# Pooled attention with two gated MLPs on one core: single steps moved in a written order of 2840 steps

## The chip, the cores and the metric

The program runs on one core of one Trainium2 chip. The metric is device time in microseconds (us) from launch to end. The core has a matrix engine (TensorE, PE in the profile), a vector engine (VectorE, DVE), a scalar engine (ScalarE, ACT), a general engine (GpSimd, POOL) and SyncE (SP), which here only issues DMAs. Each works through its own list of instructions; semaphores tie the lists together.

## The reference

q, k and v are 8 batches x 8 heads x 576 tokens x 64. Softmax attention over 8-fold pooled keys and values is followed by two gated MLPs:

```python
k_p = k.reshape(B, H, Sp, pool, D).mean(axis=3); v_p = ...   # 576 keys become 72
x = softmax(scale * q @ k_p^T) @ v_p                          # to (8, 576, 512)
h = np.maximum(x @ w_in, 0.0)                                 # 512 -> 1024
conv_out = 3-tap convolution of h along the tokens            # conv_w
x2 = (h * sigmoid(conv_out)) @ w_out                          # 1024 -> 512
h = gelu(x2 @ w_in2); u, v = h[..., :512], h[..., 512:]       # 512 -> 1024
v_s = einsum('ts,bsd->btd', w_sg, layer_norm(v) * g_ln) + b_sg
out = x2 + (u * v_s) @ w_out2                                 # 512 -> 512
```

All of it is fp32. Some weights arrive as 64-bit words, which DVE turns into fp32.

## The kernel before

Nearly every matrix product is made of three matmuls: each fp32 operand is split into a high part (a cast on ACT) and a low part (a subtraction, line L154, on POOL or DVE), and high x high, low x high and high x low are added in PSUM.

The work is written as small Python generators ("tasks"), and each `yield` ends a step of one to a dozen instructions. A key names a task: a letter, an index, and for most a batch or chunk after the dot. The text `ORDER` (line 23) holds 2840 keys; the last loop walks it and advances the named task by one step each time:

```python
for key in ORDER.split():
    step(key)
```

`step` also ties each new instruction to the one before it on the same engine, so each engine's list is exactly what `ORDER` gives. An instruction whose input is late holds all that stands behind it on its engine.

The tasks of which this text speaks; `X:n` means step n of task X:

- `s(t,b)`: scores of token tile t, batch b. PE (L438), a POOL memset of two columns of `e` (L445, step 1), DVE maximum and subtraction in two halves (L449, L454), ACT exp (L459), DVE sum (L461), POOL normalisation (L476, L480), then a DMA to DRAM.
- `e(t,b)`: the transposed probabilities. For b of 2 and more: DMA back, DVE transpose (L518), ACT cast `eTh` (L522), POOL subtraction `eTl` (L154, step 3), and DVE for a remainder. `a(p,b)`: probabilities times V (PE L117 into `psa`, ACT L550, DVE L552). `V(b)`: pooled V, of which step 3 is the ACT cast `VR` (L384). `k`, `v`: pooling on POOL (L271 to L275). `q`, `p`, `K`: loads and transposes.
- `I(f,c)`: first matmul of hidden block f (0 to 7) and token chunk c (0 to 11, 384 tokens each): 12 matmuls into a `psi` bank (L117); ACT relu and centre tap (L577, L587); DVE other taps (L589, L590); ACT tanh (L592); DVE `g` (L596); ACT cast `hg` (L599); POOL subtraction `hg` (L154). There are two `psi` banks, taken in turn, so a block's matmuls wait for `g` of the block two before it.
- `O(f,c)`: second matmul, 9 matmuls into three `pso` banks (L110 to L112). With f = 7 the banks are emptied by ACT (L623), DVE (L621), ACT, and stored to `x2s` in DRAM.
- `i`, `t`, `w`, `l`: weight blocks of the four matrices. Each is a DMA, three DVE conversions (L166, L169, L172), an ACT cast (L229) and a subtraction (L154, POOL or DVE).
- `g(i)`: block i of `w_sg`: two DMAs into `wn` (L652, L653), two PE transposes into `psa` (L659), each with an ACT cast `w2sh` (L664) and a DVE subtraction `w2sl` (L154). The last is `g4`.
- `y`, `r`: transposes of x2 for the second MLP; `n`: its v half (L760 to L769), first `n0.0`; `u`: its u half; `d`: spatial product; `m`: residual load; `o`: output product (lines from L835).

By time: chunks c = 0 and 1 with the loading of all weights run to about 155 us; chunks and batches then overlap to 575 us; the second MLP runs from there.

Of the kernel before, what the change touches and what calls it, by code (L numbers as in the profile page):

```python
# [26 lines left out]
def pooled_attention_gated_mlps(  # L27
# [25 lines left out]
    B, H, S, D = q.shape  # L53
# [46 lines left out]
    def ps_tile():  # L100
        return ps2["p"].tile([128, 2, 512], F32, tag="ps", name="ps")
# [7 lines left out]
    def mm3(out_, ah, al, bh, bl, first, last):  # L109
        nc.tensor.matmul(out=out_, lhsT=ah, rhs=bh, start=first, stop=False)  # L110
        nc.tensor.matmul(out=out_, lhsT=al, rhs=bh, start=False, stop=False)  # L111
        nc.tensor.matmul(out=out_, lhsT=ah, rhs=bl, start=False, stop=last)  # L112
# [120 lines left out]
    wi, wo, wo2, w2 = {}, {}, {}, {}  # L233
# [478 lines left out]
    g2 = {}  # L712
# [16 lines left out]
    def rows(dst, b, tiles, buf):  # L729

        if tiles[0] < NM:
            r = dst[b][128 * tiles[0]:128 * tiles[-1] + 128, :].rearrange("(j p) d -> p j d", p=128)
            return [(buf[:, 0:len(tiles), :], r)]
        return [(buf[REM * e:REM * e + REM, 0, :], dst[b - 1 + e][128 * NM:S, :]) for e in range(2)]
# [7 lines left out]
    def tiles_of(i):  # L742
        return list(range(2 * i, min(2 * i + 2, NM + 1)))
# [81 lines left out]
    ress = {}  # L825
# [9 lines left out]
    def t_o2(i, b):  # L835
        tiles = tiles_of(i)
        res = ress.pop((b, i))
        ps = ps_tile()
        for j, i in enumerate(tiles):
            T = slice(128 * i, 128 * i + 128)  # L840
            for f in range(NU):
                mm3(ps[:, j, :], g2["gh"][:, f, T], g2["gl"][:, f, T], wo2[f][:, 0, :], wo2[f][:, 1, :],
                    f == 0, f == NU - 1)
        yield
        nt = len(tiles)
        ob = outp.tile([128, 2, 512], F32, tag="ob", name="ob")
        nc.vector.tensor_tensor(out=ob[:, 0:nt, :], in0=ps[:, 0:nt, :], in1=res[:, 0:nt, :], op=ALU.add)
        yield
        for s_, d in rows([out[bb * S:bb * S + S, :] for bb in range(B)], b, tiles, ob):
            nc.sync.dma_start(out=d, in_=s_)  # L850
# [11 lines left out]
    def step(key):  # L862

        if key not in running:
            i, _, b = key[1:].partition(".")
            running[key] = iter(tasks[key[0]](int(i or 0), int(b or 0)) or ())
        more = next(running[key], 0)
        issued = nc.cur_bb.bb.instructions
        for n in range(seen[0], len(issued)):
            ins = issued[n]  # L870
            if ins.engine in last:
                tc.add_manual_dep(ins, last[ins.engine], pin, reason="order")
            last[ins.engine] = ins.name
        seen[0] = len(issued)
        return more is None

    for key in ORDER.split():
        step(key)
# [30 lines left out]
```

## Time and profile before

| | us |
|---|---|
| median of 3 runs | 1011.91 |
| lowest and highest of these | 1010.51 and 1012.82 |
| profiled execution, device time | 1010.28 |
| profiled execution, span from first to last instruction | 1008.5 |
| PE busy in the span | 960.3 (95%) |
| DVE, ACT, POOL busy | 661.7, 466.9, 371.3 |

The profile has one record for each instruction with its start, its duration, and, where its engine sat idle before it, how long and which instruction of another engine ended the wait. A duration of a PE record includes its way through the array, so the pace of PE is the distance between starts. PEclk, or the granted clock, is the share of TensorE's full 2.4 GHz that it had in a stretch; a half is 1.2 GHz.

### The profile page before, as it was taken

What the parts mean: (1) busy time and instruction counts of PE and PEld (TensorE: products, weight loads), DVE (VectorE), ACT (ScalarE), POOL (GpSimd) and SP (SyncE); (2) the same over time, 40 slices, a digit from 0 to 9 for tenths busy, and PEclk for the clock granted to TensorE, in tenths of its full rate; (3) what the DMA queues carried; (4) which work ended last, traced back from release to release, by engine and by line L of the source; (5) the groups of instructions that cost most, each with busy time, mean ns of one, the idle gap of its engine ahead of it and who ended that gap; (6) DMA issues with size and microseconds to landing.
All of it is one profiled execution on the core that took longest, in us unless ns stands there. A gap on an engine that the chain in (4) does not pass through costs nothing.

```text
span 1008.5 us, 15021 instructions
## 1 busy us (share of the span) xinstructions
PE 960.3 (95%) x5473; PEld 865.7 (86%) x5473; DVE 661.7 (66%) x1190; ACT 466.9 (46%) x908; POOL 371.3 (37%) x485
## 2 busy tenths in 40 slices
PE   5798899999998999999899899999999999999997
PEld 4687689889897898988899789898989898989896
DVE  5979986978777587796488676456364626373433
ACT  3666566777766567676456443222132313131120
POOL 3688787678777576474122100001000100010000
PEclk9899999999999999999999999999999999999999
DMA  9945273555638245141820823324141323132112
GB/s 240 308 158 95 79 173 102 124 160 137 178 100 161 75 135 138 47 126 32 230 74 1 235 55 47 107 37 107 30 109 32 76 70 88 45 64 74 42 42 63
DMA packets 210150, 105.81 MB, mean 105 GB/s; under 512 B 161472, under 2 KB 180188, under 8 KB 210076
## 3 DMA queue, kind: packets, MB, share of 16 engines
q1 hardware_dynamic: 210076, 104.85, 41.2%
q8 instruction: 43, 0.70, 0.3%
q14 instruction: 31, 0.25, 0.1%
HBM read 75.33 MB, written 29.49 MB: 104 GB/s over the span
## 4 chain that ended last, share of the span: by engine, by line
PE 76%; DVE 3%; POOL 2%; issue 2%; ACT 1%; DMA 1%; SPq 0%; POOLq 0%; DVEq 0%; ACTq 0%
PE ps L123 22%; PE psi L117 14%; PE ps L110 6%; PE ps L111 6%; PE ps L112 6%; PE pso L110 5%; PE pso L112 5%; PE pso L111 5%; PE psa L117 3%; PE psa L438 2%; DMA eds<-en 1%; POOL eTl L154 1%; POOL hg L154 1%; DVE psi L589 1%; ACT eTh L522 0%
## 5 line engine op out<-in xcount | busy, mean ns | idle before, releaser
L769 POOL TENSOR_SCALAR rstd<-mv 128x2 f32<-128x2 f32 (+1 forms) x20 | 8.9, 446 | 371.8 <-DVE mv L766 371.8
L154 POOL TENSOR_TENSOR hg<-g,hg 128x384 fp32r<-128x384 f32 x96 | 98.2, 1025 | 123.0 <-ACT hg L599 120.4
L815 DVE SCALAR_TENSOR_TENSOR y<-ps,coef,bsg 128x576 f32<-128x576 f32 x32 | 26.1, 816 | 116.2 <-PE ps L123 116.2
L589 DVE SCALAR_TENSOR_TENSOR psi<-h,coef,psi 128x384 f32<-128x384 f32 x96 | 58.6, 611 | 55.3 <-ACT psi L587 55.1
L123 PE MATMUL ps<-w2sh,v 128*128 128x288 f32 x512 | 94.3, 296 | 0.0
L820 ACT CAST gt<-y 128x576 fp32r<-128x576 f32 (+2 forms) x48 | 23.0, 512 | 117.8 <-DVE y L817 117.8
L123 PEld LDWEIGHTS ps<-w2sh,v 128*128 128x128 f32 x512 | 77.1, 189 | 0.0
L577 ACT ACTIVATE h<-psi 128x386 f32<-128x386 f32 (+1 forms) x96 | 47.2, 492 | 62.9 <-PE psi L117 62.6
L592 ACT ACTIVATE psi<-psi 128x384 f32<-128x384 f32 x96 | 45.2, 472 | 46.3 <-DVE psi L590 46.2
L154 POOL TENSOR_TENSOR eTl<-xb,eTh 128x512 fp32r<-128x512 f32 (+1 forms) x30 | 50.4, 1679 | 40.4 <-ACT eTh L522 39.1
L590 DVE SCALAR_TENSOR_TENSOR psi<-h,coef,psi 128x384 f32<-128x384 f32 x96 | 59.8, 623 | 3.4
L599 ACT CAST hg<-g 128x384 fp32r<-128x384 f32 x96 | 48.3, 506 | 26.2 <-DVE g L596 22.2
L438 PE MATMUL psa<-KBT,qT 128*128 128x144 f32 (+1 forms) x320 | 54.7, 302 | 5.5 <-DVE KBT L317 1.5
L596 DVE SCALAR_TENSOR_TENSOR g<-psi,h 128x384 f32<-128x384 f32 x96 | 52.0, 544 | 10.3 <-ACT psi L592 6.9
L587 ACT ACTIVATE psi<-h,coef 128x384 f32<-128x384 f32 x96 | 56.3, 586 | 3.1
L438 PEld LDWEIGHTS psa<-KBT,qT 128*128 128x128 f32 (+1 forms) x320 | 46.4, 187 | 12.1 <-ACT qT L420 2.5
L123 PE MATMUL ps<-w2sl,v 128*128 128x288 f32 x256 | 54.8, 296 | 0.0
L801 ACT ACTIVATE u<-ps 128x576 f32<-128x576 f32 x32 | 20.8, 653 | 64.2 <-PE ps L123 64.2
L765 DVE BATCH_NORM_STATS2 st<-vg 128x6 f32<-128x512 f32 x36 | 24.4, 678 | 36.9 <-ACT vg L760 36.9
L449 DVE TENSOR_REDUCE mx<-psa 128x4 f32<-128x288 f32 (+1 forms) x80 | 35.6, 446 | 16.7 <-PE psa L438 16.1
L522 ACT CAST eTh<-xb 128x768 fp32r<-128x768 f32 (+1 forms) x30 | 41.8, 1393 | 4.2 <-DVE xb L518 4.2
L271 POOL TENSOR_TENSOR raw<-raw 128x512 f32<-128x512 f32 (+1 forms) x36 | 40.3, 1120 | 3.5 <-DMA raw<-in_k_dram 1.7
(410 smaller groups left out, 3006.5 us busy)
## 6 DMA issues: line engine op xcount, KB each, us to landing
xb<-eds SPq DMA_DIRECT2D x24, 384.0 KB, 3.2
xb<-x2s SPq DMA_DIRECT2D x128, 72.0 KB, 2.3
x2s<-ob SPq DMA_DIRECT2D x32, 256.0 KB, 3.1
res<-x2s SPq DMA_DIRECT2D x16, 512.0 KB, 4.4
out_dram<-ob SPq DMA_DIRECT2D x16, 512.0 KB, 3.1
raw<-in_v_dram SPq DMA_DIRECT2D x54, 128.0 KB, 2.8
qb<-in_q_dram SPq DMA_DIRECT2D x96, 72.0 KB, 2.9
raw<-in_k_dram SPq DMA_DIRECT2D x12, 512.0 KB, 3.8
```

Source lines behind the costliest of these rows:

```text
L110: nc.tensor.matmul(out=out_, lhsT=ah, rhs=bh, start=first, stop=False)
L111: nc.tensor.matmul(out=out_, lhsT=al, rhs=bh, start=False, stop=False)
L112: nc.tensor.matmul(out=out_, lhsT=ah, rhs=bl, start=False, stop=last)
L117: nc.tensor.matmul(out=out_, lhsT=a, rhs=b_, start=(i == 0), stop=(i == n - 1))
L123: nc.tensor.matmul(out=ps[:, hf, 0:HS], lhsT=a, rhs=b_[:, hf * HS:(hf + 1) * HS], start=(i == 0), stop=(i == n - 1),)
L154: eng.tensor_tensor(out=out, in0=in0, in1=hi.bitcast(F32), op=ALU.subtract)
L438: nc.tensor.matmul(out=ps[0:n, 2 * SP * x:2 * SP * x + 2 * SP], lhsT=qT[:, p, 0:n], rhs=KBT[:, p, :], start=True, stop=True)
L587: nc.scalar.activation(out=y, in_=tap(1), func=AF.Copy, scale=cw(1, f))
L589: nc.vector.scalar_tensor_tensor(out=y, in0=tap(0), scalar=cw(0, f), in1=y, op0=ALU.mult, op1=ALU.add)
L590: nc.vector.scalar_tensor_tensor(out=y, in0=tap(2), scalar=cw(2, f), in1=y, op0=ALU.mult, op1=ALU.add)
L596: nc.vector.scalar_tensor_tensor(out=go, in0=y, scalar=1.0, in1=tap(1), op0=ALU.add, op1=ALU.mult)
L599: nc.scalar.copy(out=hg[:, 0, f, :], in_=g)
```

## The change

`ORDER` holds the same 2840 keys, the same number of each, in another order. One more edit makes this possible at the end of the kernel: `t_o2` takes its residual tile out of the table after its matmuls instead of before, so that the `m` step that loads it may stand behind the `o` step that issues the matmuls. No instruction is added, taken away or given another shape.

```diff
-ORDER = '''z k0.0 k1.0 k2.0 z z p0.0 c p1.0 p2.0 v0.0 v1.0 p3.0 p4.0 v2.0 i0 i1 z z k0.1 k0.1 k1.1 ...
+ORDER = '''z k0.0 k1.0 k2.0 z z p0.0 c p1.0 p2.0 v0.0 v1.0 p3.0 p4.0 v2.0 i0 i1 z z k0.1 v1.1 i2 ...
...
     def t_o2(i, b):
         tiles = tiles_of(i)
-        res = ress.pop((b, i))
+        k = (b, i)
         ps = ps_tile()
...
         yield
         nt = len(tiles)
+        res = ress.pop(k)
         ob = outp.tile([128, 2, 512], F32, tag="ob", name="ob")
```

What stands where is read from the two built programs, of which four places follow (a number behind a name is its buffer).

**ACT, ahead of `I0.6`.** Before: psi_3617 is block I6.5, psi_3649 is I7.5, psi_3701 is I0.6.

```order
L577 ACTIVATE h_3645<-psi_3617 128x386
L587 ACTIVATE psi_3617<-h_3645,coef_115 128x384
L459 ACTIVATE e_3586<-e_3586 128x8x72
L384 CAST VR_128<-vrm_3664 96x512
L577 ACTIVATE h_3678<-psi_3649 128x386
L587 ACTIVATE psi_3649<-h_3678,coef_115 128x384
L522 CAST eTh_129<-xb_3594 128x6x128
L592 ACTIVATE psi_3617<-psi_3617 128x384
L592 ACTIVATE psi_3649<-psi_3649 128x384
```

Now, with psi_3597 for I6.5, psi_3623 for I7.5 and psi_3678 for I0.6:

```order
L599 CAST hg_558<-g_3590 128x384
L592 ACTIVATE psi_3597<-psi_3597 128x384
L577 ACTIVATE h_3658<-psi_3623 128x386
L587 ACTIVATE psi_3623<-h_3658,coef_115 128x384
L522 CAST eTh_129<-xb_3619 128x6x128
L592 ACTIVATE psi_3623<-psi_3623 128x384
L599 CAST hg_558<-g_3654 128x384
L623 ACTIVATE ob_3703<-pso_3172 128x512
L623 ACTIVATE ob_3711<-pso_3174 128x512
L577 ACTIVATE h_3732<-psi_3678 128x386
L587 ACTIVATE psi_3678<-h_3732,coef_115 128x384
L384 CAST VR_128<-vrm_3656 96x512
```

The tanh (L592) of I6.5 moved ahead of I7.5's first ACT pair and of the `eTh` cast, and the `VR` cast (V.5:3) moved behind the first pair of I0.6. On PE the 9 matmuls of `O7.4` moved from ahead of I6.5 to between I7.5 and I0.6.

**PE, ahead of `I0.10`** (wi7hl is I7.9, wi0hl is I0.10). Before:

```order
L117 MATMUL psi<-xl,wi7hl 128x386
L117 MATMUL psi<-xh,wi7hl 128x386
L117 MATMUL psi<-xh,wi0hl 128x388
L117 MATMUL psi<-xl,wi0hl 128x388
L117 MATMUL psi<-xh,wi0hl 128x388 x2
```

Now, with the middle of the two groups `O0.9` and `O1.9` left out:

```order
L117 MATMUL psi<-xh,wi7hl 128x386
L110 MATMUL pso<-w0hl,hg 128x512
L111 MATMUL pso<-w0hl,hg 128x512
...
L112 MATMUL pso<-w1hl,hg 128x512
L117 MATMUL psi<-xh,wi0hl 128x388
```

The 18 matmuls of `O0.9` and `O1.9` moved from behind I1.10 to ahead of I0.10; ahead of I7.9 there now stand three groups `a` (12 matmuls) instead of one.

**DVE, ahead of `n0.0`** (w2sl is written by `g`; t, w4 to w7 belong to the weights `l0` to `l3`). Before:

```order
L621 TENSOR_SCALAR ob_6245<-pso_6073 128x512
L166 TENSOR_SCALAR t_6251<-w4raw_6200 128x512
L154 TENSOR_TENSOR x2l1_6121<-xt_6238,x2h1_6120 128x576
L169 SCALAR_TENSOR_TENSOR t_6251<-w4raw_6200,t_6251 128x512
L166 TENSOR_SCALAR t_6256<-w5raw_6213 128x512
L172 SCALAR_TENSOR_TENSOR t_6251<-w4raw_6200,t_6251 128x512
L169 SCALAR_TENSOR_TENSOR t_6256<-w5raw_6213,t_6256 128x512
L154 TENSOR_TENSOR w2sl_5383<-psa_6258,w2sh_5382 128x4x64
L172 SCALAR_TENSOR_TENSOR t_6256<-w5raw_6213,t_6256 128x512
L154 TENSOR_TENSOR w4hl_6266<-t_6251,w4hl_6266 128x512
L154 TENSOR_TENSOR w2sl_5383<-psa_6269,w2sh_5382 128x64
```

Now:

```order
L154 TENSOR_TENSOR w2sl_5387<-psa_6225,w2sh_5386 128x128
L621 TENSOR_SCALAR ob_6240<-pso_6076 128x512
L154 TENSOR_TENSOR w2sl_5387<-psa_6242,w2sh_5386 128x4x64
L154 TENSOR_TENSOR w2sl_5387<-psa_6251,w2sh_5386 128x64
L166 TENSOR_SCALAR t_6270<-w5raw_6221 128x512
L169 SCALAR_TENSOR_TENSOR t_6270<-w5raw_6221,t_6270 128x512
```

Both subtractions of `g4` now stand ahead of all conversions of `l0` and `l1`; on ACT both casts of `g4` stand ahead of theirs as well. On PE `g2:4` moved from behind O5.11 to ahead of it, on SP the `wn` load of `g4` ahead of the load of `l1`.

**POOL, around the scores `s0.4`.** Before, the two memsets are those of s0.4 and s1.4, and eTl<-xb_2561 is e3.3:

```order
L445 MEMSET e_2620 128x8
L445 MEMSET e_2630 128x8
L154 TENSOR_TENSOR hg_563<-g_2624,hg_563 128x384
L154 TENSOR_TENSOR hg_563<-g_2634,hg_563 128x384
L154 TENSOR_TENSOR eTl_130<-xb_2561,eTh_129 128x4x128
```

Now, with eTl<-xb_2533 for e3.3:

```order
L271 TENSOR_TENSOR raw_2610<-raw_2610 64x256
L154 TENSOR_TENSOR eTl_130<-xb_2533,eTh_129 128x4x128
L445 MEMSET e_2641 128x8
L445 MEMSET e_2661 128x8
L154 TENSOR_TENSOR hg_558<-g_2615,hg_558 128x384
```

The memsets moved behind the subtraction of e3.3. Elsewhere too single steps of all kinds stand earlier or later on all five engines. In the first 155 us DVE has the conversions of weight t1 ahead of I0.0's `g` instead of behind it, and POOL the pooling `v0.3:1` behind instead of ahead of weight t6's subtraction. Near 269 us `O6.3` moved on PE from ahead of I5.4 to behind it, so that `O6.3` and `O7.3` stand between I5.4 and I6.4 instead of `O7.3` alone.

## Rows read from the trace of the kernel before

**Rows 1.** The page: busy time by engine, and chain that ended last by engine.

```profile
PE 960.3 (95%) x5473; PEld 865.7 (86%) x5473; DVE 661.7 (66%) x1190; ACT 466.9 (46%) x908; POOL 371.3 (37%) x485
PE 76%; DVE 3%; POOL 2%; issue 2%; ACT 1%; DMA 1%; SPq 0%; POOLq 0%; DVEq 0%; ACTq 0%
```

**Rows 2.** Waits of PE: us in total, times, longest.

```profile
PE psi L117 <- DVE g L596: 10.1, 6, 3.7
...
PE pso L112 <- POOL w6hl L154: 3.4, 1, 3.4
```

**Rows 3.** Windows: stretch, length, busy us (records) by engine, clock, DMA share, GB/s.

```profile
100.00:125.00 25.00, 20.37 (x116) 17.24 (x116) 24.09 (x46) 15.12 (x35) 18.96 (x25) 0.98 0.29 79
...
155.00:305.00 150.00, 148.08 (x807) 133.71 (x807) 117.53 (x231) 104.04 (x205) 114.52 (x143) 1.00 0.51 130
...
495.00:565.00 70.00, 70.00 (x351) 62.77 (x350) 53.22 (x89) 39.17 (x79) 16.26 (x16) 1.00 0.33 87
...
590.00:1000.00 410.00, 409.49 (x2499) 376.70 (x2498) 206.88 (x336) 103.89 (x172) 22.88 (x40) 1.00 0.26 63
```

**Rows 4.** Windows around four waits, columns as in Rows 3.

```profile
121.00:131.00 10.00, 6.56 (x20) 5.45 (x21) 8.94 (x16) 2.53 (x5) 9.85 (x13) 0.66 0.53 137
321.00:325.00 4.00, 4.00 (x15) 3.54 (x16) 1.75 (x4) 1.84 (x4) 3.92 (x6) 0.59 1.15 239
488.00:492.00 4.00, 3.89 (x14) 3.89 (x15) 0.61 (x2) 1.46 (x4) 1.97 (x2) 0.63 1.12 312
...
581.50:589.00 7.50, 7.46 (x27) 6.07 (x28) 4.96 (x9) 1.46 (x3) 0.00 (x0) 0.79 0.32 61
```

**Rows 5.** Timeline ahead of I0.6: start, duration, operation, idle time before it.

```profile
316.05 0.62 DVE L590 SCALAR_TENSOR_TENSOR psi<-h,coef,psi 128x384 f32<-128x384 f32 x1
...
318.17 1.51 ACT L522 CAST eTh<-xb 128x768 fp32r<-128x768 f32 x1
319.57 0.85 ACT L592 ACTIVATE psi<-psi 128x384 f32<-128x384 f32 x2
...
320.94 0.45 PE L117 MATMUL psi<-xh,wi0hl 128*128 128x386 f32 x1 [3.69 <-DVE g L596]
```

**Rows 6.** Timeline of PE at I6.4.

```profile
268.99 0.44 PE L117 MATMUL psi<-xh,wi6hl 128*128 128x388 f32 x1 [1.37 <-DVE g L596]
```

**Rows 7.** Timelines ahead of I0.10.

```profile
487.51 0.55 DVE L596 SCALAR_TENSOR_TENSOR g<-psi,h 128x384 f32<-128x384 f32 x1
...
488.11 0.45 PE L117 MATMUL psi<-xh,wi0hl 128*128 128x388 f32 x1 [2.97 <-DVE g L596]
```

**Rows 8.** Timelines ahead of n0.0.

```profile
576.97 0.49 PE L659 MATMUL psa<-ident,wn 64*128 64x64 f32 x5 [1.52 <-DMA wn<-in_moe_w_sg_dram]
...
577.44 0.37 ACT L664 CAST w2sh<-psa 128x256 fp32r<-128x256 f32 x1 [0.63 <-PE psa L659]
...
580.26 0.20 ACT L664 CAST w2sh<-psa 128x64 fp32r<-128x64 f32 x1
...
581.27 0.22 DVE L154 TENSOR_TENSOR w2sl<-psa,w2sh 128x64 fp32r<-128x64 f32 x1
...
581.54 0.79 PE L110 MATMUL ps<-w201hl,x2h 128*128 128x512 f32 x1 [4.07 <-DVE w2sl L154]
```

**Rows 9.** Timelines of POOL, DVE and PE around s0.4.

```profile
229.21 1.96 POOL L154 TENSOR_TENSOR eTl<-xb,eTh 128x512 fp32r<-128x512 f32 x1
...
227.85 0.46 DVE L454 TENSOR_TENSOR e<-psa,mx 128x288 f32<-128x288 f32 x1
...
229.16 0.61 DVE L154 TENSOR_TENSOR eTh<-xb,eTh 32x256 fp32r<-32x256 f32 x1 [0.48 <-ACT eTh L522]
...
231.33 0.66 PE L438 MATMUL psa<-KBT,qT 128*128 128x144 f32 x4
```

**Rows 10.** Timelines of DVE and POOL in the first 155 us.

```profile
63.48 0.38 DVE L317 COPY KBT<-psa 64x216 f32<-64x216 f32 x1 [3.22 <-ACT KBT L315]
...
118.99 3.54 POOL L154 TENSOR_TENSOR Vl<-vp,Vh 32x256 fp32r<-32x256 f32 x4
```

2 lines of the change are left out of this document (1 added, 1 removed).

## The prediction

> **What bounds the kernel now.** I read the page first. PE is busy for 960.3 of 1008.5 us, no other engine for more than 66%, and the chain of work that ended last lies on PE for 76% of the span [rows 1]. Equal work in another order can therefore win only what PE loses, some 48 us of idle time and the time at half clock; it can also lose, where PE is now fed in time. The table of windows says where that is. From 155 to 305 us PE idles 2 of 150 us, from 495 to 565 none, from 590 to 1000 half a microsecond of 410 [rows 3]. So the second MLP, 40% of the time, has nothing to give. In the first 155 us DVE is the limit: from 100 to 125 it is busy for 24.1 of 25 us while PE idles 4.6 [rows 3]. What remains are single waits. PE's waits show that the largest steady cause is a `psi` bank that is not free because `g` is late: 10.1 us in 6 waits [rows 2]. Behind a long wait stands a second loss. The granted clock is 0.59 from 321 to 325 us, 0.63 from 488 to 492, 0.79 from 581.5 to 589 [rows 4], each time just after an idle stretch of PE of 3 to 4 us; it is 1.00 from 155 to 305 us, in which the longest wait that I name is 1.37 us [rows 3, 6].
>
> **The change part by part.** Added and removed work is nothing, so the sum has only waits in it, made against the profiled execution's 1010.3 us, which is 1.6 below the median.
>
> (a) Ahead of I0.6 PE idles 3.69 us for the `g` of I6.5 [rows 5]. The tanh of I6.5 had its input from DVE at 316.7 (316.05 + 0.62) and ran at 319.57, since the `VR` cast, a pair of I7.5 and the 1.51 us `eTh` cast stood ahead of it on ACT [rows 5]. That is 2.9 us of standing in line. Now it stands ahead of these, and nine matmuls of `O7.4` stand between I7.5 and I0.6, which puts the need later too. In the stretch from 495 to 565, where PE never idles, 351 records take 70 us, 0.199 us each [rows 3]; nine are at least 1.8 us, an estimate. Supply 2.9 earlier, need 1.8 later: 4.7 against a wait of 3.69, so it goes, and I take all of it. With it goes the half clock, 4 x (1 - 0.59) = 1.6 us [rows 4]. Gain 5.3. What is late next is the `VR` cast, now behind I0.6's pair; its readers are the `a` groups of the next chunk, later on PE than I0.6.
>
> (b) Ahead of I6.4 PE idles 1.37 us [rows 6]. `O6.3` now lies between I5.4 and I6.4, again 1.8 us of cover. Gain 1.4.
>
> (c) Ahead of I0.10 PE idles 2.97 us; the `g` it waits for ends at 487.51 + 0.55 = 488.06 [rows 7]. Now 18 matmuls of `O0.9` and `O1.9`, at least 3.6 us by the same pace, stand between I7.9 and I0.10. Their operand is `hg` of blocks long done. Gain 3.0, and 4 x (1 - 0.63) = 1.5 of clock [rows 4]: 4.5.
>
> (d) Ahead of n0.0 PE waits 1.52 us for `wn`, then 4.07 us for the last subtraction of `g4` [rows 8], and then runs at 0.79: 7.5 x 0.21 = 1.6 us [rows 4]. Together 7.2. Now the casts and subtractions of `g4` stand ahead of the conversions of `l0` and `l1`, and the `wn` load can start earlier since `g2:4`, which frees its buffer, moved ahead of O5.11. But nothing was put between `g4`'s transposes and n0.0, so the bare chain stays: 0.49 on PE, casts of 0.37 and 0.20, a subtraction of 0.22 [rows 8], 1.3, and about 1.5 with what lies between them. Gain 5.7; its bounds are 2.5, if `wn` is no earlier and the clock falls as before, and 7.2.
>
> (e) Around s0.4 the change makes a wait. The memset of `e` stands behind e3.3's subtraction on POOL, which ended at 229.21 + 1.96 = 231.2; the DVE step that writes `e` after it ran at 227.85 [rows 9]. DVE will stand there until 231.2, and behind it queue the rest of itself (0.46), e3.3's remainder (0.61) and s1.4's pair (twice 0.46, as for s0.4), done at 233.2. PE went on to second score halves at 231.33 [rows 9] and now has to wait for that pair first: 1.9, I take 2.0. Bounds 0, if POOL comes to e3.3 earlier, and 3.3, the whole delay of DVE.
>
> (f) The first 155 us. DVE idles 3.22 us ahead of one KBT copy [rows 10], and the conversions of weight t1 now stand in that hole. POOL's 3.54 us of `Vl` subtractions still stand ahead of weight t6 [rows 10], for which PE waits 3.4 [rows 2]; only `v0.3:1` left that line. Against these stands a memset that moved behind another POOL step, like (e). With DVE busy at 24.1 of 25 us a PE wait that goes there comes back as another. I take 0, with bounds of a gain of 3.4 + 10 x (1 - 0.66) = 6.8 [rows 2, 4] and a loss of 4, two waits like (e).
>
> (g) Everything else that moved has no row. The nearest is the remainder of the `psi` waits: 10.1 less 3.69, 2.97 and 1.37 is 2.1 us in three places [rows 2, 5 to 7]. Several blocks now have less PE work between I(n) and I(n+2) than before, so I take a loss of that size, 2.1; bounds a gain of 2.1, if these go too, and a loss of 5.3, one more place like (a).
>
> The sum: 5.3 + 1.4 + 4.5 + 5.7 = 16.9 won, 2.0 + 2.1 = 4.1 lost, net 12.8. 1010.3 - 12.8 = 997.5, and with 1.6 for the median 999.1.
>
> **The rivals.** *Waits move rather than go.* Two `psi` banks remain, so a need that is not covered in one place appears in another; the many shortened distances between I blocks speak for it, the amount of cover in (a) and (c) against. If half of the 16.9 comes back: 1011.9 - 8.4 + 4.1 = 1007.6.
>
> *The front gains as well.* The holes of DVE [rows 10] are filled, t6 comes earlier, and (e) is covered: 999.1 - 6.8 - 2.0 = 990.3. Against it speaks DVE's 24.1 of 25 us.
>
> *Slower: POOL as a line in which everything stands.* POOL is busy for 114.5 of 150 us from 155 to 305 [rows 3]. The new order puts memsets and low-part subtractions behind, or ahead of inputs to, steps that are not ready. Place: every batch from 2 to 7 has five scores whose memset can stand as in (e). Price: 2.0 each, and where two meet, a PE wait of near 4 us with 1.6 of clock as in (a): 5.6. Three such meetings make 16.8 and eat the gain whole; from there on it is slower, and with the 4.1 already counted the time is 1011.9 - 16.9 + 4.1 + 16.8 = 1015.9. That POOL idles for a quarter of that stretch speaks against it. The Trainium skill, "TensorE: Matmul & The Clock Gate", section "Architectural detail", calls the queues of ACT, DVE and GpSimd strict first in, first out, which is this rival's rule; the tanh that stood 2.9 us behind other casts [rows 5] agrees.
>
> *The clock falls all the same.* The 4.7 us of clock in (a), (c) and (d), 1.6 + 1.5 + 1.6 [rows 4], come back, because what is left of idle time there, or the waits of (e), still brings half clock: 999.1 + 4.7 = 1003.8. The 1.00 from 155 to 305 us beside a wait of 1.37 [rows 3, 6] speaks against. The Trainium skill, "TensorE: Matmul & The Clock Gate", section "What's actually happening", says that for modelling the ramp penalty is under 1% of a typical kernel's span, and that one should not fit it; by that rule I would leave the same terms out and come to the same 1003.8. The 0.59 in rows 4 speaks for counting them.
>
> *It does nothing.* PE's busy time is the same, and only the named waits change; if (a) and (c) find other late inputs, 1011.9.
>
> **How the numbers follow.** Forecast 0.50, the clock falls all the same 0.06, waits move 0.14, front gains 0.09, slower 0.14, nothing 0.07. The predicted time is the forecast's, 999. The range goes from 989, the front case, to 1012, nothing; the forecast's own bounds, from (d) at 2.5, (e) at 3.3 and (g) at 5.3, reach 1006.8, and below, with (g) at -2.1 and (d) at 7.2, 993.4. A measurement of this kernel can tell about 0.2%, 2 us, from no change. Faster by more: 0.50 + 0.06 + 0.14 + 0.09, less 0.01 for the edge of the third, 0.78; within: 0.08; slower: 0.14.
>
> **What would show it.** In the profile after, PE's waits on `g` should fall from 10.1 to under 4 us, with no gap above 2 us ahead of I0.6 and I0.10 and a clock of 1.00 in both places. Ahead of n0.0 a wait of about 1.5 us should remain and none for `wn`. Around s0.4 DVE should idle some 3 us for POOL's memset, and PE some 2. The time at 155 us, counted by the end of chunk 1, should move by less than 4. A row of PE waits of 2 us or more on POOL between 155 and 480 us, or half clock at new places, would make the prediction wrong on the slow side; a front shorter by 6, on the fast side.

## The result and the profile after

| | before | changed |
|---|---|---|
| median, 4 runs each (us) | 1011.96 | 996.48 |
| lowest and highest | 1010.51, 1012.82 | 995.61, 997.89 |
| profiled execution: device time, span | 1010.28, 1008.5 | 996.36, 994.6 |

The ratio is 0.9849, with a 95% interval of 0.9837 to 0.9862: 15.5 us less, where 12.8 less (999) was predicted.

The page of the changed kernel gives busy time by engine. The counts of instructions are those of [rows 1]; busy time differs by 2.1 us on PE, 8.2 on DVE and 6.6 on ACT.

```profile
PE 958.2 (96%) x5473; PEld 864.4 (87%) x5473; DVE 669.9 (67%) x1190; ACT 460.3 (46%) x908; POOL 371.0 (37%) x485
```

PE's waits in the changed kernel (total, times, longest), against [rows 2]: the wait of `psi` for `g` falls from 10.1 to 2.3 us, the one for w6's low part from 3.4 to 0.5. In the first 155 us the wait for KBT grew from 1.5 to 3.4 us, and waits for `eTl` and `xl` are new or longer.

```profile
PE psa L438 <- DVE KBT L317: 3.4, 1, 3.4
PE psa L507 <- DVE eTl L154: 2.6, 2, 2.2
PE psa L438 <- DVE xl L552: 2.4, 2, 1.9
PE psi L117 <- DVE g L596: 2.3, 4, 1.0
...
PE pso L112 <- POOL w6hl L154: 0.5, 1, 0.5
```

Windows of the changed kernel (busy us and records for PE, PEld, DVE, ACT, POOL; clock; DMA share; GB/s). They answer to [rows 3] and [rows 4]: PE is full from 305 to 325 and from 476 to 495 us, at a clock of 1.00, where before it lost the waits of I0.6 and I0.10 and ran at 0.59 and 0.63 behind them; from 565 to 590 it idles 1 us. The losses left are in the first 155 us.

```profile
50.00:75.00 25.00, 20.43 (x140) 19.05 (x140) 18.07 (x30) 11.93 (x26) 21.56 (x25) 0.86 0.59 172
...
100.00:125.00 25.00, 19.96 (x114) 16.99 (x114) 23.60 (x44) 14.06 (x33) 14.12 (x20) 1.00 0.22 59
155.00:305.00 150.00, 149.35 (x810) 134.37 (x810) 125.32 (x237) 102.47 (x205) 115.79 (x145) 1.00 0.53 137
305.00:325.00 20.00, 20.00 (x109) 17.98 (x108) 17.56 (x35) 15.34 (x27) 14.53 (x20) 1.00 0.76 129
...
476.00:495.00 19.00, 19.00 (x102) 17.51 (x101) 10.59 (x21) 10.37 (x24) 5.03 (x5) 1.00 0.79 174
...
565.00:590.00 25.00, 23.96 (x132) 20.63 (x131) 19.68 (x41) 11.57 (x22) 3.23 (x5) 1.00 0.62 160
```

Where the time went is seen best from the start of the same block's first matmul in both traces:

| first matmul of | before | changed | difference | change in this stretch |
|---|---|---|---|---|
| O7.1 | 181.81 | 186.06 | +4.3 | +4.3 |
| O7.3 | 265.37 | 269.72 | +4.4 | +0.1 |
| O7.5 | 354.64 | 351.45 | -3.2 | -7.5 |
| O7.9 | 516.95 | 509.16 | -7.8 | -4.6 |
| n0.4 | 779.63 | 765.34 | -14.3 | -6.5 |
| o0.7 | 988.93 | 975.17 | -13.8 | +0.5 |

So 18.6 us are won in three stretches, and the first 155 us give some back: 4.3 against this one execution of before. Part of that 4.3 is chance. Kernels with before's own first 155 us start e0.0, at 19 to 21 us, up to 2 us apart in their profiles, and the one shown in [rows 1 to 10] is an early one. Eight profiles of kernels that have before's order up to there reach O7.1 at 181.7 to 184.3 us, 183.2 in the mean; the two that have the changed order up to there, this one and f4_memset below, reach it at 186.1 and 185.0. By these, and by the run f1_front155 below, the front costs about 2.

### The profile page after: what moved, and what is told of

It is laid out like the page before. It is cut to its first block, busy times and chain, and to the rows that moved or that the text cites. A ratio compares the mean times of both kernels' runs of the same rounds, so it can differ in the third digit from the quotient of the medians.

```text
span 994.6 us, 15039 instructions
## 1 busy us (share of the span) xinstructions
PE 958.2 (96%) x5473; PEld 864.4 (87%) x5473; DVE 669.9 (67%) x1190; ACT 460.3 (46%) x908; POOL 371.0 (37%) x485
## 4 chain that ended last, share of the span: by engine, by line
PE 80%; DVE 7%; DMA 4%; POOL 3%; issue 2%; ACT 2%; SPq 2%; DVEq 0%; POOLq 0%; ACTq 0%
PE ps L123 22%; PE psi L117 16%; PE ps L110 7%; PE ps L111 7%; PE ps L112 7%; PE pso L110 5%; PE pso L112 5%; PE pso L111 5%; PE psa L117 3%; PE psa L438 3%; DMA st<-in_v_dram 1%; SPq L411 1%; POOL eTl L154 1%; DMA st<-in_k_dram 1%; DMA raw<-in_k_dram 1%
## 5 line engine op out<-in xcount | busy, mean ns | idle before, releaser
L769 POOL TENSOR_SCALAR rstd<-mv 128x2 f32<-128x2 f32 (+1 forms) x20 | 6.8, 340 | 361.3 <-DVE mv L766 361.0
L592 ACT ACTIVATE psi<-psi 128x384 f32<-128x384 f32 x96 | 45.3, 474 | 56.2 <-DVE psi L590 56.0
L154 POOL TENSOR_TENSOR eTl<-xb,eTh 128x512 fp32r<-128x512 f32 (+1 forms) x30 | 47.1, 1572 | 50.2 <-ACT eTh L522 50.1
L438 PEld LDWEIGHTS psa<-KBT,qT 128*128 128x128 f32 (+1 forms) x320 | 46.3, 189 | 17.4 <-DVE KBT L317 3.6
L848 DVE TENSOR_TENSOR ob<-ps,res 128x1024 f32<-128x1024 f32 (+1 forms) x20 | 22.2, 1112 | 34.7 <-PE ps L112 34.7
L476 POOL TENSOR_TENSOR en<-e,rs 128x512 f32<-128x512 f32 (+1 forms) x30 | 32.7, 1091 | 29.9 <-DVE rs L463 14.1
```

Source lines behind the costliest of these rows:

```text
L154: eng.tensor_tensor(out=out, in0=in0, in1=hi.bitcast(F32), op=ALU.subtract)
L438: nc.tensor.matmul(out=ps[0:n, 2 * SP * x:2 * SP * x + 2 * SP], lhsT=qT[:, p, 0:n], rhs=KBT[:, p, :], start=True, stop=True)
```

## The experiments

In the diffs a line is one engine's list, with X:n for step n of task X; what is not shown stays in place.

### Ahead of I0.6: one queue at a time

**g1_tanh**, on the order of before:

```diff
-ACT: I6.5:1 s3.5:5 V.5:3 I7.5:1 e1.5:2 I6.5:3 ... I0.6:1 s4.5:5
+ACT: I6.5:1 I6.5:3 s3.5:5 I7.5:1 e1.5:2 ... I0.6:1 V.5:3 s4.5:5
-POOL: V.5:4 e1.5:3 ... I7.5:6
+POOL: e1.5:3 ... I7.5:6 V.5:4
```

> The order of before with ScalarE's steps ahead of I0.6 alone moved: the tanh of I6.5 ahead of I7.5's first pair, the VR cast behind I0.6's first pair. TensorE's order untouched. The wait before I0.6 was 3.69 us, and 1.6 us of half clock followed. Theory A, the tanh stood in line for 2.9 us and that is what the wait is made of: the wait falls to some 1 us, no half clock, 1012 - 2.7 - 1.6 = about 1007.7. Rival B, VectorE's g of I6.5 is held by what stands ahead of it on VectorE (e1.5's remainder, which needs the eTh cast): the wait stays, 1012.

1014.16 us, ratio 1.0016 (1.0006 to 1.0025): nothing won, and some 1.6 us lost. Timeline of this kernel on ACT, DVE and PE:

```profile
318.48 0.47 ACT L592 ACTIVATE psi<-psi 128x384 f32<-128x384 f32 x1 [1.54 <-DVE psi L590]
...
320.48 1.50 ACT L522 CAST eTh<-xb 128x768 fp32r<-128x768 f32 x1
...
322.01 0.58 DVE L154 TENSOR_TENSOR eTh<-xb,eTh 32x256 fp32r<-32x256 f32 x1 [0.16 <-ACT eTh L522]
322.62 1.02 DVE L596 SCALAR_TENSOR_TENSOR g<-psi,h 128x384 f32<-128x384 f32 x2
...
323.33 0.55 PE L117 MATMUL psi<-xh,wi0hl 128*128 128x386 f32 x1 [4.30 <-DVE g L596]
```

The tanh now runs as soon as its input is there (318.48), but `g`, which reads it, comes at 322.62: ahead of it on DVE stands e1.5's remainder, and that needs the `eTh` cast, done at 322.0. The wait, 3.69 before and 4.30 now, passed from one queue to the next. Rival B holds.

**g2_o74**, on the order of before:

```diff
-PE: O7.4 I6.5 s3.5:3 I7.5 s4.5:0 I0.6
+PE: I6.5 s3.5:3 I7.5 O7.4 s4.5:0 I0.6
-ACT: O7.4:1 ... O7.4:5
+ACT: ... O7.4:1 O7.4:5
```

> The order of before with the nine matmuls of O7.4 alone moved from ahead of I6.5 to between I7.5 and I0.6 (and ScalarE's first eviction of O7.4 to just ahead of its second). ScalarE's other order untouched. Theory A, nine matmuls (2.0 us) are cover: the block I6.5 starts 2.0 earlier and I0.6 need not start earlier, so the whole chain has 2.0 us more, and the wait falls from 3.69 to about 1.6 with or without half clock: 1008.3 to 1010. Rival B, cover alone suffices since ScalarE's queue starts earlier as well: the wait goes, about 1006.5.

1013.04 us, ratio 1.0006 (0.9995 to 1.0017). PE's rows with a wait in this stretch:

```profile
316.14 0.44 PE L117 MATMUL psi<-xh,wi7hl 128*128 128x386 f32 x1 [1.21 <-DVE g L596]
323.44 0.44 PE L117 MATMUL psi<-xh,wi0hl 128*128 128x386 f32 x1 [2.23 <-DVE g L596]
```

1.21 + 2.23 = 3.44 in place of 3.69. Taking O7.4 from ahead of I6.5 takes cover from I7.5 (which waits for I5.5's `g`) and gives it to I0.6. Theory A's 1.6 at I0.6 was near, but it had not counted what the cover had covered before; the time stays.

**k2_actdve**, g1 with one more step:

```diff
-DVE: I6.5:2 e1.5:1 s3.5:6 I7.5:2 e1.5:4 I6.5:4 I7.5:4
+DVE: I6.5:2 e1.5:1 I6.5:4 s3.5:6 I7.5:2 e1.5:4 I7.5:4
```

> The order of before with the tanh of I6.5 ahead on ScalarE and its g ahead on VectorE (in front of I7.5's taps and e1.5's remainder), VR back; TensorE's order untouched. With ScalarE alone moved the wait before I0.6 was 4.30 us, because g stood behind e1.5's remainder, which stands behind the eTh cast. Theory A: both queues together take away 2.5 us or more of the 3.69, and no half clock follows: 1012.2 - 4 = 1008. Rival B: without O7.4 as cover the chain of I6.5 itself (pair, taps, tanh, g, some 3.4 us against 2.8 us of matmuls) leaves over 2 us: 1010 or more.

1012.61 us, ratio 1.0004 (0.9993 to 1.0016). PE's waits, and a window behind them:

```profile
319.28 0.44 PE L117 MATMUL psi<-xh,wi0hl 128*128 128x386 f32 x1 [0.80 <-DVE g L596]
323.83 0.50 PE L110 MATMUL pso<-w0hl,hg 128*128 128x512 f32 x1 [0.63 <-ACT ob L623]
336.50 0.40 PE L117 MATMUL psa<-eTh,Vh 128*128 128x288 f32 x1 [0.59 <-ACT eTh L522]
338.46 0.40 PE L117 MATMUL psa<-eTl,Vh 128*128 128x288 f32 x1 [1.56 <-POOL eTl L154]
...
336.00:345.00 9.00, 6.94 (x28) 5.91 (x29) 4.85 (x9) 3.97 (x9) 6.26 (x7) 0.81 0.30 68
```

Both queues together do what theory A said at the place itself: 3.69 falls to 0.80, without half clock. But the time is not kept. The eviction of O7.4 and the `eTh` cast, which now stand behind, are what O0.5 and a0.5 wait for, and in the window with the last two waits the clock is 0.81, 9 x 0.19 = 1.7 us. Won 2.9 + 1.6, given back 0.63 + 0.59 + 1.56 - 0.38 + 1.7 = 4.1 within 25 us (0.38 is what a0.5 waited before). This is the prediction's rival "waits move rather than go", in this form of the edit.

**w_window**: before up to I2.4 (245 us), then the 397 steps up to O7.5 that the change has there, in its order, then as before.

```diff
-ORDER: before[.. I2.4:0]  before[.. O7.5:0]   before[rest]
+ORDER: before[.. I2.4:0]  changed[.. O7.5:0]  before[rest]
```

> The order of before up to I2.4 (245 us), then the some 400 steps up to O7.5 (355 us) in the changed order, then all as before. The few steps at I0.6 alone took its wait away but gave the time back within 20 us, to the wait of a0.5 for the eTl of e1.5 and of O0.5 for an eviction. Theory A: what makes the gain of this stretch last is the other moved steps of the same stretch: 7.5 us less by O7.5, nothing elsewhere, 1004.5. Rival B: the stretch draws on a lead of VectorE and GpSimd that the changed order builds before 245 us, or hands its late work on behind 355 us: 1008 or more.

1007.89 us, ratio 0.9963 (0.9952 to 0.9975), which is 3.7 less. From O7.3 to O7.5 it gains 7.5 against before, exactly what the change gains there, at a clock of 1.00. It loses some 1.7 at each end, where one order meets the other:

```profile
259.47 0.45 PE L117 MATMUL psi<-xh,wi4hl 128*128 128x388 f32 x1 [1.71 <-DVE g L596]
355.59 0.37 PE L117 MATMUL psa<-eTh,Vh 128*128 128x288 f32 x1 [1.33 <-DVE e L454]
...
245.00:355.00 110.00, 107.41 (x572) 95.61 (x571) 86.79 (x160) 74.01 (x146) 80.90 (x101) 1.00 0.56 134
```

So the gain at I0.6 is made within the stretch, as theory A said, and the few steps nearest the wait do not make it; which of the other moved steps do was not taken apart. The total is the rival's 1008 and not theory A's 1004.5. Whether the two losses at the ends come from the seams alone or from a lead that the changed order builds up earlier, as the rival has it, this run cannot tell.

### Ahead of I0.10

**g4_i010**, on the order of before:

```diff
-PE: I7.9 I0.10 I1.10 O0.9 O1.9
+PE: I7.9 O0.9 O1.9 I0.10 I1.10
-ACT: I6.9:5 I7.9:5 I0.10:1 O7.8:5
+ACT: I6.9:5 O7.8:5 I7.9:5 I0.10:1
```

> The order of before with the matmuls of O0.9 and O1.9 moved ahead of I0.10, and with them the last eviction of O7.8, whose bank O1.9's chunk takes. Theory A: 18 matmuls cover the wait of 2.97 us, and the 1.5 us of half clock go: 1012 - 4.5 = 1007.5. Rival B: I2.10 and I3.10 now follow I0.10 and I1.10 with 18 matmuls less between them, so the same wait stands there: 1012.

1012.13 us, ratio 1.0000 (0.9991 to 1.0010). PE and ACT in this kernel:

```profile
491.42 0.80 PE L110 MATMUL pso<-w0hl,hg 128*128 128x512 f32 x1 [2.63 <-ACT ob L623]
...
490.77 0.59 ACT L623 ACTIVATE ob<-pso 128x512 f32<-128x512 f32 x1
```

Neither theory named what happened: O0.9's third `pso` bank is emptied by the last eviction of O7.8, which ACT reaches at 490.77, behind the cast of I6.9. The time is the rival's 1012, for another reason than the rival's. The wait of 2.97 before I0.10 became one of 2.63 within O0.9.

**k1_three**, on the order of before: g2 and k2 together at I0.6; at I0.10 the edit of g4 with the last two evictions of O7.8 right behind I5.9's cast; ahead of n0.0 the edit of g3 below with two more steps.

```diff
-ACT: I5.9:5 I6.9:1 ... I6.9:5 I7.9:5 I0.10:1 O7.8:5
+ACT: I5.9:5 O7.8:5 I6.9:1 ... I6.9:5 I7.9:5 I0.10:1
-DVE: I5.9:2 O7.8:3 a0.7:5 I5.9:4 a1.7:5 a2.7:5
+DVE: I5.9:2 a0.7:5 I5.9:4 a1.7:5 O7.8:3 a2.7:5
-PE: g2:1 O5.11 g2:4 O6.11
+PE: g2:1 g2:4 O5.11 O6.11
-SP: l1:0 g4:0
+SP: g4:0 l1:0
```

> The order of before with three places set as the change has them, and nothing else: ahead of I0.6 the tanh and g of I6.5 and the nine matmuls of O7.4, all together; ahead of I0.10 the 18 matmuls of O0.9 and O1.9 and, unlike in the run of these alone, the last two evictions of O7.8 early on ScalarE; ahead of n0.0 g4's subtractions ahead of l0 and l1, g2's second transpose ahead of O5.11 and the load of g4 ahead of that of l1. Theory A: each place needs its steps together, since the wait passes from one queue to the next, and these some twenty steps carry the whole gain after 155 us: 5.3, 4.5 and 6 us less, about 996. Rival B: the gain needs the hundreds of other moved steps that make room on ScalarE, VectorE and GpSimd: 1002 or more, with waits of over 2 us left in these places.

1002.49 us, ratio 0.9918 (0.9898 to 0.9938): 8.3 less by the ratio, 9.5 by the two medians. PE rows with a wait, and windows at the three places:

```profile
315.69 0.44 PE L117 MATMUL psi<-xh,wi7hl 128*128 128x386 f32 x1 [1.22 <-DVE g L596]
324.52 0.50 PE L110 MATMUL pso<-w0hl,hg 128*128 128x512 f32 x1 [0.80 <-ACT ob L623]
339.19 0.40 PE L117 MATMUL psa<-eTl,Vh 128*128 128x288 f32 x1 [1.56 <-POOL eTl L154]
...
480.00:500.00 20.00, 20.00 (x106) 18.51 (x105) 10.32 (x19) 10.59 (x23) 4.99 (x5) 1.00 0.86 245
565.00:590.00 25.00, 22.78 (x123) 19.39 (x122) 17.47 (x36) 10.26 (x18) 1.01 (x3) 1.00 0.61 154
```

By the starts of blocks, 1.5 us are won from O7.3 to O7.5, 4.7 from O7.8 to O7.9, 4.8 from O7.11 to n0.4. With the eviction moved as well, PE is full from 480 to 500 us and I0.10 gives all that the change gives there (4.6). So some twenty steps carry the second place and most of the third (4.8 of 6.5); the first needs its neighbourhood. The total is what rival B gave, 1002 or more, and a wait of 2.2 us is left ahead of n0.0; theory A holds for the second place and for most of the third.

### Ahead of n0.0

**g3_join**, on the order of before:

```diff
-DVE: O7.11:3 l0:1 y0.1:3 l0:2 l1:1 l0:3 l1:2 g4:3 l1:3 l0:5 g4:6
+DVE: O7.11:3 y0.1:3 g4:3 g4:6 l0:1 l0:2 l1:1 l0:3 l1:2 l1:3 l0:5
-ACT: g4:2 l0:4 O7.11:5 g4:5
+ACT: g4:2 O7.11:5 g4:5 l0:4
```

> The order of before with the conversions, cast and subtraction of weights l0 and l1 moved behind the last subtraction of g4; nothing else. Before, TensorE waited 1.52 us for the load of wn, then 4.07 us for that subtraction, and 1.6 us went to half clock. Theory A: the load wait stays, the second wait falls to about 1.5, half clock may stay: 2.6 to 4.2 us less, 1008 to 1009.5. Rival B, the conversions now come too late for the second MLP's first output blocks and the gain is given back: 1012.

1009.44 us, ratio 0.9972 (0.9962 to 0.9983), which is 2.8 less (1.7 to 3.8), theory A. PE's waits, and the window behind them:

```profile
576.67 0.49 PE L659 MATMUL psa<-ident,wn 64*128 64x64 f32 x5 [1.29 <-DVE ob L621]
578.42 0.79 PE L110 MATMUL ps<-w201hl,x2h 128*128 128x512 f32 x1 [1.26 <-DVE w2sl L154]
...
578.40:589.00 10.60, 10.58 (x34) 8.52 (x35) 8.82 (x16) 4.44 (x6) 0.00 (x0) 0.72 0.38 104
```

4.07 fell to 1.26, as the change's bare chain should. The wait ahead of g4's transposes stayed (1.52 before, 1.29 now), and the clock is still 0.72 behind them: in this profile n0.4 comes 1.7 us sooner after O7.11, though the two waits are 3.0 shorter. k1_three, with `g2:4` and g4's load moved, loses the 1.29 and the half clock (1.00 from 565 to 590) and keeps a wait of 2.2 us ahead of n0.0. The late conversions of l0 and l1 hold nobody up: rival B is out.

### Around s0.4

**f4_memset**, on the changed order:

```diff
-POOL: e3.3:3 s0.4:1 s1.4:1 I5.3:6
+POOL: s0.4:1 s1.4:1 e3.3:3 I5.3:6
```

> The changed order with the memsets of s0.4 and s1.4 moved on POOL back to ahead of e3.3's subtraction. The prediction's step (e) said their place behind it costs 2.0 us: by that theory about 994.5. The trace after shows VectorE's pair of s0.4 at 232.50, ahead of the memset at 235.60, so by the rival theory that pair never waits for the memset (it writes other columns; only the sum that follows reads both) and the move is worth nothing: 996.5, within 0.7 us.

996.42 us, ratio to before 0.9856 (0.9842 to 0.9871), against 0.9849 for the change: worth nothing. The changed kernel's rows say why:

```profile
235.60 0.16 POOL L445 MEMSET e<- 128x8 f32 x2
...
232.98 0.46 DVE L454 TENSOR_TENSOR e<-psa,mx 128x288 f32<-128x288 f32 x1
```

The memset is as late as predicted, but the DVE step that writes `e` ran 2.6 us ahead of it. The memset fills the last column of each head in `e`, L454 the others; only the later sum reads both.

### The first 155 us

**f1_front155** has the order of before up to I7.1:6, then the changed one.

```diff
-ORDER: changed[.. I7.1:6]  changed[rest]
+ORDER: before[.. I7.1:6]   changed[rest]
```

> The changed order with the first 155 us (up to the last step of I7.1) put back as it was before; the rest as changed. By the traces the changed order reaches the same matmuls 4.3 us later at O7.1 (186.06 against 181.81) and is 3.2 us ahead by O7.5. Theory A, the first 155 us cost 4.3 us by themselves and the later gains do not hang on them: 996.5 - 4.3 = about 992. Rival B, the late start is what gives later engines their lead (DVE, ACT and POOL have done more by then), so the lost time is paid back later: about 996.5, with new waits between 155 and 330 us.

993.93 us, ratio 0.9830 (0.9816 to 0.9845): some 2 us less than the change, though the intervals overlap a little. The gains after 155 us are all there (O7.1 at 184.36, o0.7 at 973.41: 18.1 us against before), so theory A is right that they don't hang on the front, and the front costs about 2, not 4.3. This kernel's e0.0 started at 21.3 us, where the one profiled execution of before had 19.4 with the same order.

**f2_front65**: the same with the cut at s0.1:0 (64 us).

```diff
-ORDER: changed[.. s0.1:0]  changed[rest]
+ORDER: before[.. s0.1:0]   changed[rest]
```

> The changed order with only the part up to the first scores of chunk 1 (s0.1, at 64 us before and 66.6 us after) put back. Of the 4.3 us, 2.6 stand at that place in the traces and 1.7 come after. Theory A: about 994, 2.6 less than the changed order. Rival B (all of it comes from 25 to 65 us, the later part only shows the conversions that were put off): about 992, as much as the whole front. Rival C: the DVE work put off comes back as a wait between 65 and 155 us, and nothing is won: 996.5.

998.59 us, ratio 0.9875 (0.9860 to 0.9889): slower than the change by some 2.6. A wait of 4.5 us of PE for POOL's `en` stands at 79.5 us; neither parent has it, so the seam makes it. It does not tell the theories apart, beyond that a cut in this stretch is itself dear.

**f3_kbt**, on the changed order:

```diff
-DVE: I0.0:2 t1:1 t1:2 t1:3 t0:3 K.1:6
+DVE: I0.0:2 K.1:6 t1:1 t1:2 t1:3 t0:3
```

> The changed order with one step moved: the copy of KBT on VectorE (K.1:6) directly behind the ScalarE half of it, ahead of the conversions of weights t1 and t0 instead of behind them. In the changed trace that copy ended at 66.6 us though its input was there at 62.1, and TensorE waited 3.41 us for it and then ran at half clock. Theory A: the wait goes, 2.5 to 4 us less, about 993.5. Rival: VectorE is the limit up to 155 us, so the conversions are late instead and another TensorE wait takes its place: within 1 us of 996.5.

995.25 us, ratio 0.9839 (0.9823 to 0.9856): 1.2 us below the change, within the noise, and nearer the rival than theory A's 993.5. First the wait in the kernel before, from the same table as [rows 2]; then rows of the changed kernel; then PE and a window of f3_kbt:

```profile
PE psa L438 <- DVE KBT L317: 1.5, 1, 1.5
```

```profile
61.92 0.16 ACT L315 COPY KBT<-psa 64x8 f32<-64x8 f32 x1
...
62.01 0.42 DVE L166 TENSOR_SCALAR t<-w1raw 128x512 uint32<-128x512 uint32 x1
...
63.60 1.63 DVE L172 SCALAR_TENSOR_TENSOR t<-w1raw,t 128x512 uint32<-128x512 uint32 x1
65.15 0.94 DVE L172 SCALAR_TENSOR_TENSOR t<-w0raw,t 128x512 uint32<-128x512 uint32 x1
66.12 0.38 DVE L317 COPY KBT<-psa 64x216 f32<-64x216 f32 x1
...
66.55 1.09 PE L438 MATMUL psa<-KBT,qT 128*128 128x144 f32 x3 [3.41 <-DVE KBT L317]
```

```profile
68.54 0.63 PE L416 MATMUL psa<-ident,qb 128*128 128x128 f32 x4 [1.14 <-issue]
71.28 0.73 PE L438 MATMUL psa<-KBT,qT 128*128 128x144 f32 x4 [1.24 <-DVE e L451]
...
100.00:125.00 25.00, 21.43 (x112) 19.30 (x111) 22.30 (x42) 13.32 (x32) 13.31 (x19) 0.86 0.18 52
```

In the changed kernel there was no hole left to fill. ACT's part of KBT was done at 62.1 (61.92 + 0.16), and DVE came free at just that time; before, DVE had idled until 63.48 [rows 10]. The four conversions, of which three rows stand here, then held the copy until 66.12, and PE waited 3.41 us for it, 1.9 more than before. With the copy first, that wait is gone and 1.14 + 1.24 take its place.

**k3b**, on f1: the three conversions of t1 into before's hole, and weight t6's subtraction ahead of V.2's on POOL.

```diff
-DVE: I0.0:4 K.1:6 t1:1 s0.1:2 t1:2 t1:3
+DVE: I0.0:4 t1:1 t1:2 t1:3 K.1:6 s0.1:2
-POOL: V.2:1 v0.3:1 t6:5
+POOL: v0.3:1 t6:5 V.2:1
```

> The changed order with the first 155 us as before (993.9 in that run), and two moves in it: the three conversions of weight t1 into VectorE's idle 3.2 us ahead of the KBT copy, and the subtraction of weight t6 ahead of the Vl subtractions of V.2 on GpSimd, for which TensorE waited 3.4 us and then ran at half clock for some 5 us. Theory A: the two holes are what the front loses; about 2 us for the first and 2.4 + 2.5 for the second: 988 to 990. Rival B: VectorE is the limit of the front, t6's conversions come no earlier, and the wait for them only changes its name: 992 to 994.

994.13 us, ratio 0.9828 (0.9810 to 0.9845), the same as f1: rival B. PE's waits in this kernel:

```profile
65.04 0.76 PE L438 MATMUL psa<-KBT,qT 128*128 128x144 f32 x4 [2.83 <-DVE KBT L317]
...
123.00 0.50 PE L110 MATMUL pso<-w6hl,hg 128*128 128x512 f32 x1 [1.07 <-ACT w6hl L229]
124.35 0.50 PE L112 MATMUL pso<-w6hl,hg 128*128 128x512 f32 x1 [0.62 <-POOL w6hl L154]
```

The 3.4 us for w6 fell to 1.07 + 0.62, but O7.0 then waits 1.26 for w7 and I5.1 1.77 for `g` (1.12 in f1), and the copy of KBT is late behind t1 again (2.83, in f1 1.47). Two holes of the front were filled, and no gain shows; one below some 2 us would not.

## Why the prediction was right, point by point

- **What bounds the kernel: right.** Work is unchanged; what moved is PE's waits and the half clock behind them. From 590 us on nothing was won, and the last stretch loses 0.5.
- **(a) and (b), I0.6 and I6.4: the sum right, its reason wrong.** 5.3 + 1.4 = 6.7 predicted, 7.5 measured from O7.3 to O7.5. The other 0.8 is two waits for `eTl`, 0.40 us at 276 and 0.38 at 339, for which the prediction had no term and which are gone too. The step that failed is "supply 2.9 earlier, need 1.8 later". It followed one queue, ACT; g1 shows that DVE's order held `g` just as long, g2 that the cover had been covering I7.5, k2 that even with the wait gone the delayed `eTh` cast and eviction take the time back. w_window shows that the stretch as a whole makes the gain. What made the sum come out was the other moved steps, which the prediction had not read. One of them is on DVE: in the changed order `g` of I6.5 stands ahead of e1.5's remainder, which has moved behind I0.6. That the sum came out is thus luck in part.
- **(c), I0.10: size right, 4.5 predicted, 4.6 measured.** The step "their operand is hg of blocks long done" was not enough: the output bank has to be free too, which g4 (nothing) and k1 (4.7) show. The change had moved that eviction; the prediction did not look.
- **(d), n0.0: 5.7 predicted, 6.5 measured.** The `wn` wait is gone, the clock is 1.00, and 1.03 us of the predicted 1.5 remain. They end on an ACT eviction and not on g4's subtraction, as this row of the changed kernel says:

```profile
569.05 0.47 PE L110 MATMUL ps<-w201hl,x2h 128*128 128x512 f32 x1 [1.03 <-ACT ob L623]
```

- **(e), s0.4: wrong, 0 instead of 2.0.** The failed step is "the DVE step that writes `e` after it": the two write different columns of one tile, and nothing orders them.
- **(f), the front: 0 taken, about 2 lost,** within its bounds of a gain of 6.8 and a loss of 4; its sign, under 4 us at the end of chunk 1, reads 4.3 at O7.1 in the two profiles of the result. The conversions "now stand in that hole" was the step that failed: in the changed kernel the copy's input is there as soon as DVE is free, the conversions only delay it, and PE waits 3.41 us in place of 1.5. The wait for w6 fell from 3.4 to 0.5, but that is no gain: w6's subtraction on POOL ends later than before, at 131.4 in place of 125.1 us, and PE comes to it later still. That a repaired wait comes back as another there, f3 and k3b show. That DVE is the limit of the whole front is more than the row for 100 to 125 us says: from 50 to 75 it is busy for 18.1 of 25 us in the changed kernel.
- **(g), the rest: 2.1 taken as loss, 0 seen** from 155 us to 590, within its bounds; 0.5 in the last stretch. The row that sized it was misread: the three other waits for `g` stand in the first 155 us, which (f) already covers. Two of them in the kernel before (the third, at 144.6, is 0.18):

```profile
92.67 0.44 PE L117 MATMUL psi<-xh,wi6hl 128*128 128x386 f32 x1 [0.80 <-DVE g L596]
...
141.43 0.45 PE L117 MATMUL psi<-xh,wi5hl 128*128 128x388 f32 x1 [1.13 <-DVE g L596]
```

- **The clock: counted, and rightly.** At all three places it is 1.00 now. Without its terms the sum would have been 1003.8, as that rival says, where 996.5 was measured. g3 shows the reverse: its waits are 3.0 us shorter, but the clock behind them is 0.72, and its profile gains only 1.7 there.

The miss of 2.5 us is thus 2.0 of (e), 2.1 of (g), 0.8 of (a) and (b) and 0.8 of (d), less 2 of (f) and the 0.5 of the end; this makes 3.2, and the 0.7 between is less than two executions differ by. That it is so small is luck in part: 4.1 us of loss that did not come stood against the loss of the front, which had been put at nothing.

## What to carry to other kernels

A wait that a queue's order makes is rarely made by one queue: before a gain is booked, follow the waiting operand back through every engine's list, and look at what stood in the place that the moved step takes, and at the output bank as well as the input. The order of two writes to one tile says nothing about a wait; read which columns they touch. A hole in the old trace need not be there in the new order: before work is put into it, ask when the input that ends the hole will come, and whether the engine is free before that.

## What was not expected of the hardware

- Half clock does not follow from the length of a wait alone. In the changed kernel PE waits 2.19 us at 106 us, and the clock is 1.00 from 100 to 125; in f3_kbt the same wait stands at 104.7, and the clock is 0.86 in the same window. Around a wait of 1.56 us, with one of 0.59 us shortly ahead of it, k2_actdve shows 0.81 from 336 to 345 us; with the 1.56 alone k1_three shows 1.00 in the same window. What decides stayed open. The waits in the changed kernel and in f3_kbt, and the window of k1_three:

```profile
105.98 0.38 PE L507 MATMUL psa<-ident,en 128*32 128x128 f32 x2 [2.19 <-DVE eTl L154]
...
104.65 0.38 PE L507 MATMUL psa<-ident,en 128*32 128x128 f32 x2 [2.19 <-DVE eTl L154]
...
336.00:345.00 9.00, 7.44 (x42) 6.55 (x41) 5.51 (x10) 5.05 (x10) 7.02 (x7) 1.00 0.30 68
```

- Programs with the same order in the first 155 us differ by some 2 us there from one profiled execution to the next. In g2_o74's profile 16 matmuls that pool `v` (sums over an identity matrix) take 3.48 us at 17.4 us, in that of before 1.95, at 16.4 us, while the clock column shows 1.00 from 14 to 22 us in both:

```profile
17.42 3.48 PE L117 MATMUL psa<-st,ident 128*128 128x128 f32 x16
...
16.39 1.95 PE L117 MATMUL psa<-st,ident 128*128 128x128 f32 x16
```

So single profiles of two orders can be compared only from a common block on, and totals by medians.
